# RWKV-5 and SwiGLU on one core: scores in four 64-column tiles, with half of the heads in swapped halves of time

## The chip, the cores and the metric

The kernel runs on one core of one Trainium2 chip. A core has five engines that run beside each other: TensorE (PE in the profile; PEld are its weight loads), VectorE (DVE), ScalarE (ACT), GpSimd (POOL) and SyncE (SP), whose queue issues most of the DMA transfers. They meet through semaphores. SBUF and PSUM have 128 partitions[...]. The metric is the time of one execution on the device, in microseconds, as the median of several runs. The time before is 603.12 us, the median of three (602.46 to 603.63).

## The reference

Two parts, one after the other, all in float32. Batch 4, 8 heads, 768 steps, 48 values a head:

```
for t in range(768):                       # attention, for each batch b and head h
    cur   = (u * k[t]) outer v[t]
    y[t]  = r[t] @ (state + cur)
    state = w * state + k[t] outer v[t]    # w: one decay for each head and key index
x = y as (4*768, 8*48)                     # 3072 tokens of 384
g = x @ w_gate;  val = x @ w_val           # 384 x 1536 each
out = (g * sigmoid(g) * val) @ w_out       # 1536 x 384
```

Within 128 steps the recurrence is a masked product. With k and r scaled by powers of w, `scores[key, query] = sum_d k[key, d] r[query, d]` for key before query, plus a diagonal from u; `y = scores^T v + r @ state`.

## The kernel before, in words

**Units.** The work of attention is cut into 24 units, unit `i` being 128 steps (`c = i // 4`) of one batch (`b = i % 4`). All 8 heads of a unit stand side by side, in four pairs `a`; head `2a + e` has the partitions `64e` to `64e + 47` once it is turned.

**A unit's way.** `load` and `load_v` fetch k, r and v with step on the partition, one transfer on SP for k, one for r, two for v. POOL scales k and r with two tables, `kscale` and `rscale`, that have step on the partition (`scale_k` L307, `scale_r` L310), and makes the unscaled product of r and k for the diagonal (`own_product` L234, L235; summed on VectorE by `own_sum` L240). From unit 12 on (`BLOCKS`) turning is not TensorE's: `move_blocks` (L364) issues 16 transfers on SP that move 32x32 blocks from SBUF to SBUF into one pair of buffers, and `turn_blocks` (L379) lets VectorE transpose 32x32 blocks twice, for k and for r. There is one such pair of buffers, so the moves of the next unit wait for the transposes of this one. `scores` (L393) then multiplies keys and queries of each head, 8 matmuls of 48 rows x 128 columns of weights and 128 moving columns, the even heads into one PSUM bank and the odd heads into another; `copy_predicated` (L398, VectorE) copies what lies above the diagonal under a mask into `At`, whose diagonal ScalarE has written (L328). `outputs` (L426) multiplies with v and with the state Z, in column tiles of 32: 28 matmuls; `update` (L441) makes the state's new part.

**Order.** The order of every engine is written out by hand (`manual_schedule`): a stage `s` scales unit `s + 1`, issues its loads and those of `s + 3`, turns unit `s`, makes the scores of `s - 1` and, from stage 12 on, right behind them the outputs and the update of `s - 2`. Between these stand pieces of the feed-forward block from a list `todo`, which `gaps` spreads over the stages. In odd stages the loads of `s + 3` stand on SP ahead of the moves, in even ones (`late`) behind them. The products of the feed-forward block are TensorE's main work: gate and value at first plainly (`gate_value`, L464), from the third group on in a scheme with fewer products, 15 rounds (`three_step`, L720) whose sums and differences VectorE, ScalarE (L744, L854) and POOL (L650, L623) make; the output projection (`project`, L539) in one of seven products. `three_beside` runs these rounds between the units in PSUM banks from the list `free`, `three_units` runs them after the last unit and takes banks of the pool `ps_a` too.

**PSUM.** Eight banks: four named ones for the feed-forward block, and a pool `ps_a` of four, from which scores, outputs, updates and transposes take theirs in rotation. `copy_predicated` is put off in a list, `lazy`.

Of the kernel before, what the change touches and what calls it, by code (L numbers as in the profile page):

```python
# [22 lines left out]
def fast(  # L23
# [39 lines left out]
    ps_a = ctx.enter_context(tc.tile_pool(name="ps_a", bufs=4, space=bass.MemoryType.PSUM))  # L63
# [8 lines left out]
    bad = cst.tile([P, HP], FP32, name="bad")  # L72
    held = cst.tile([P, HP], FP32, name="held")
    badc = cst.tile([P, 1], FP32, name="badc")
    ones = cst.tile([P, 1], FP32, name="ones")
    ident = cst.tile([P, P], FP32, name="ident")
    mask = cst.tile([P, P], FP32, name="mask")
# [12 lines left out]
    free = deque(banks[:2])  # L90

# [25 lines left out]

    def load(i):
        c, b = divmod(i, B)
        rows = slice(P * c, P * (c + 1))  # L120
        for src, dst in zip((k, r), raw(i)):
            sp.dma_start(out=dst, in_=src[b, :, rows, :].rearrange("h t d -> t h d"))

    def load_v(i):
        c, b = divmod(i, B)
        rows = slice(P * c, P * (c + 1))
        for e in range(2):
            sp.dma_start(
                out=v_ld[i % 4][:, :, 64 * e : 64 * e + D],
                in_=v[b, :, rows, :].rearrange("(a e) t d -> e t a d", e=2)[e],  # L130
            )
# [133 lines left out]
    def warm(n):  # L265

        ps = ps_a.tile([P, HP, P], FP32, name="warm", tag="a")
        for _ in range(n):
            pe.matmul(ps[:, 0, :], ident[:], ident[:], start=True, stop=True)
# [6 lines left out]
        base=0, pattern=[[1, P]], channel_multiplier=-1,  # L276
    )
    dve.tensor_scalar(held[:], wcol[:], W_LOW, W_HIGH, ALU.max, ALU.min)
# [33 lines left out]
    def natural_tables():  # L312
        for t, dst in ((pw[:, :, 1 : P + 1], kscale), (pv, rscale)):
            t_ps = ps_a.tile([P, HP, P], FP32, name="t_ps", tag="a")
            for a in range(HP):
                pe.transpose(t_ps[:, a, :], t[:, a, :], ident[:])
            act.copy(dst, t_ps[:].rearrange("p a (e x) -> p (a e) x", e=2)[:, :, 0:D])
# [25 lines left out]
    def turn(i):  # L343
        kr = khat[i % 4], rhat_of(i)
        tps = [ps_a.tile([P, HP, P], FP32, name="tp", tag="a") for _ in kr]
        turned[i] = three.tile([P, HP, P], FP32, name="rT", tag="rT")
        for tp, t, dst, table in zip(tps, kr, (kT[i % 2], turned[i]), (pw[:, :, 1 : P + 1], pv)):
            for a in range(HP):
                pe.transpose(tp[:, a, :], pair(t, a), ident[:])  # L349
            if i < 4:  # L350
                dve.tensor_mul(dst[:], tp[:], table)
            else:
                act.copy(dst[:], tp[:])
# [31 lines left out]
    def scores(i):  # L385

        while lazy:
            lazy.popleft()()
        ps = [ps_a.tile([P, HP, P], FP32, name="s_ps", tag="a") for _ in range(2)]
        for a in range(HP):  # L390
            for e in range(2):
                rows = slice(64 * e, 64 * e + D)
                pe.matmul(  # L393
                    ps[e][:, a, :], kT[i % 2][rows, at(i, a), :], turned[i][rows, at(i, a), :],
                    start=True, stop=True, skip_group_check=True,
                )
        for e in range(2):
            lazy.append(lambda e=e: dve.copy_predicated(  # L398
                At[i % 2][:].rearrange("p (a e) t -> p a e t", e=2)[:, :, e],
                mask[:].bitcast(INT32).unsqueeze(1).to_broadcast([P, HP, P]), ps[e][:],  # L400
            ))
        lazy.popleft()()
        if i < BLOCKS:
            lazy.popleft()()

    def outputs(i):

        c, b = divmod(i, B)  # L410
        A, vl, z = At[i % 2], v_ld[i % 4], Z[b]
        rT = turned.pop(i)
        ps = ps_a.tile([P, CC, P], FP32, name="y_ps", tag="a")
        cols = [[] for _ in range(4)]
        for m in range(4 * CC):
            (cc, q), (a, s) = divmod(m, 4), divmod(m, 3)
            each = [(z[0:R2, a, 32 * s : 32 * s + 32], rT[0:R2, at(i, a), :])] if c > 0 else []
            if s < 2:
                each.append((vl[:, a, 32 * s : 32 * s + 32], A[:, 2 * a, :]))
            if s > 0:  # L420
                each.append((vl[:, a, 32 * s + 16 : 32 * s + 48], A[:, 2 * a + 1, :]))
            cols[q] += [(cc, x, n == 0, n == len(each) - 1) for n, x in enumerate(each)]
        for n in range(len(cols[0])):
            for q in range(4):
                cc, x, start, stop = cols[q][n]
                pe.matmul(  # L426
                    ps[32 * q : 32 * q + 32, cc, :], *x,
                    start=start, stop=stop, skip_group_check=True,
                )
        act.copy(xT[:, i % NX, :, :], ps[:])  # L430

    def update(i):
# [4 lines left out]
        ps = ps_a.tile([P, HP, D], FP32, name="u_ps", tag="a")  # L437
# [398 lines left out]
    def three_units(g):  # L836
# [8 lines left out]
        def bank(chain):  # L845
            return wide[chain][:]

        def open_(chain):
            if chain in ("l4", "l2"):
                return take()  # L850
            return ps_a.tile([P, 4 * P], FP32, name=f"c_{chain}", tag="a")

        def later(at, do, out, *args):
            todo.append((at, lambda: do(out, *(bank(a) if isinstance(a, str) else a for a in args))))  # L854

# [9 lines left out]
        for t in range(4):  # L865
# [16 lines left out]
            later(z + 9.6, act.copy, y, "y")  # L882
            later(z + 10.4, dve.tensor_add, c[5], q10, "l5")
            later(z + (11.55 if t == 3 else 10.5), dve.tensor_add, c[2], y, "l1")
# [3 lines left out]
            later(z + r4, dve.tensor_sub, c[1], "l1", x)  # L888
            later(z + r4 + 0.1, dve.tensor_sub, c[1], c[1], "l8")
            later(z + r0, dve.tensor_sub, c[2], c[2], "l2")  # L890
            todo.append((z + r0 + 0.05, lambda: free.append(wide["l2"])))
            later(z + 11.6, dve.tensor_sub, c[0], r12, "n")
            silu(z + 10.8, 0, room["c"][:, 2], hTs[:, :, 3 * t + 2], pool, z + 10.9)
# [158 lines left out]
    for s in range(4, N + 2):  # L1052
        if 4 < s < N:
            own_sum(s)
        late = BLOCKS < s + 1 < N and s % 2 == 0
        if s + 1 < N:
            scale_k(s + 1)
            if not late:
                scale_r(s + 1)
            own_product(s + 1)  # L1060
            load_v(s + 1)
            if s + 3 < N and not late:
                load(s + 3)
# [30 lines left out]
        if s == 12:  # L1094

            dve.tensor_tensor(bad[:], held[:], wcol[:], ALU.not_equal)
            dve.tensor_reduce(badc[:], bad[:], axis=AX.X, op=ALU.add)
            dve.memset(ones[:], 1.0)
            n_ps = ps_a.tile([P, HP, P], FP32, name="n_ps", tag="a")
            pe.matmul(n_ps[0:1, 0, 0:1], badc[:], ones[:], start=True, stop=True)  # L1100
            act.copy(outside, n_ps[0:1, 0, 0:1])
# [426 lines left out]
```

## Time and profile before

| | |
|---|---|
| median of the runs | 603.12 us (602.46 to 603.63) |
| the profiled execution | 602.26 us, its span 600.4 us |
| granted TensorE clock | 0.999 |
| TensorE, its weight loads | 586.4 us (98%), 528.0 us (88%) |
| VectorE, ScalarE, POOL | 404.7 us (67%), 227.8 us (38%), 312.7 us (52%) |
| scores (L393), matmuls | 384 records, 28.2 us busy |
| outputs (L426), matmuls | 768 and 480 records, 34.9 and 29.8 us busy |
| update (L441), matmuls | 640 records, 10.1 us busy |
| block moves (L364) | 192 transfers of 32 KB, 2.0 us to landing |
| loads of k, of r (k_ld, r_ld), of v | 20, 20 and 48 transfers; 3.3, 3.7 and 3.5 us to landing |

The page says for each group of instructions its line, engine and operation, what it writes and reads, its shape and number, then its busy time, the mean length of one in ns, and the idle time of the engine before it with what ended it. For TensorE "48*128 48x128" is weights of 48 rows and 128 columns and a moving operand of 48 rows and 128 columns. Matmuls are pipelined, and a row's mean length is longer than the distance from one to the next; what a stretch costs is read from the chain, which follows the last instruction back through what released it. A float32 matmul leaves two records.

### The profile page before, as it was taken

The numbers are of one execution on the slowest core, as the hardware profiler recorded it, in microseconds if no ns is written. First come the engines' busy times: TensorE is split into PE (matmuls) and PEld (weight loads), VectorE is DVE, ScalarE is ACT, GpSimd is POOL, SyncE is SP. The second block draws the span as 40 slices with busy tenths as digits, with TensorE's granted clock in tenths as the row PEclk, the third lists the DMA queues.
The fourth block names the chain that finished last, engine by engine and source line by source line (L and its number), as shares of the span: only waits on it lengthen the run. The fifth ranks groups of instructions, "written<-read, shape, count | busy, mean of one in ns | idle before, by whom it ended". The sixth has DMA issues, their size and how long they took to land.

```text
span 600.4 us, 12410 instructions
## 1 busy us (share of the span) xinstructions
PE 586.4 (98%) x4920; PEld 528.0 (88%) x4920; DVE 404.7 (67%) x682; ACT 227.8 (38%) x524; POOL 312.7 (52%) x349
## 2 busy tenths in 40 slices
PE   8799999999999999999999999999999999999996
PEld 7578888899988889988899988889988899988896
DVE  5867886359477877477869477869347686277660
ACT  3358887321353422253441244432134421243310
POOL 4879888987999501977710988404445200011000
PEclk9999999999999999999999999999999999999999
DMA  7989883241530503133251253200100000000001
GB/s 174 236 210 246 228 289 84 44 73 40 115 47 8 97 3 75 37 66 53 34 93 24 68 88 49 36 2 1 41 14 0 2 1 26 27 1 1 2 0 58
DMA packets 138003, 40.43 MB, mean 67 GB/s; under 512 B 128592, under 2 KB 131792, under 8 KB 137936
## 3 DMA queue, kind: packets, MB, share of 16 engines
q1 hardware_dynamic: 134480, 34.82, 27.3%
q10 hardware_dynamic: 3456, 4.72, 2.2%
q8 instruction: 41, 0.67, 0.5%
q14 instruction: 26, 0.21, 0.1%
HBM read 28.51 MB, written 4.72 MB: 55 GB/s over the span
## 4 chain that ended last, share of the span: by engine, by line
PE 88%; POOL 2%; DVE 2%; issue 1%; DMA 1%; ACT 0%; SPq 0%; DVEq 0%; POOLq 0%
PE bank L720 31%; PE bank L539 26%; PE bank L464 7%; PE c_l L720 6%; PE y_ps L426 6%; PE c_n L720 3%; PE c_y L720 3%; PE s_ps L393 3%; POOL wgv L222 1%; PE u_ps L441 1%; PE tp L349 1%; DMA r_ld<-in_r_dram 1%; DVE hv L744 1%; DVE hs L513 0%; POOL hats L310 0%
## 5 line engine op out<-in xcount | busy, mean ns | idle before, releaser
L744 DVE TENSOR_TENSOR hv<-hv,bank 128x512 f32<-128x512 f32 x132 | 88.1, 683 | 29.6 <-PE bank L720 19.3
L464 PE MATMUL bank<-xT,wgv 128*128 128x256 f32 x288 | 66.8, 385 | 0.6 <-ACT xT L430 0.6
L328 ACT ACTIVATE At<-ident,du 128x128 f32<-128x128 f32 x176 | 60.3, 396 | 15.6 <-DVE hv L552 7.5
L720 PE MATMUL bank<-xf,wgv 128*128 128x256 f32 x256 | 66.0, 382 | 0.0
L860 POOL TENSOR_TENSOR hv<-At,hats 128x512 f32<-128x512 f32 x8 | 10.2, 1274 | 107.1 <-ACT At L859 107.1
L744 ACT COPY hv<-bank 128x512 f32<-128x512 f32 x72 | 40.2, 585 | 59.5 <-PE bank L720 50.5
L464 PEld LDWEIGHTS bank<-xT,wgv 128*128 128x128 f32 x288 | 53.2, 190 | 8.9 <-ACT xT L430 0.8
L650 POOL TENSOR_TENSOR s<-wgv 128x256 f32<-128x256 f32 x39 | 30.0, 793 | 53.4 <-PE bank L539 53.2
L720 PEld LDWEIGHTS bank<-xf,wgv 128*128 128x128 f32 x256 | 47.8, 190 | 7.0 <-DVE kT L854 0.6
L539 PE MATMUL bank<-wo,hv 128*128 128x192 f32 x288 | 49.6, 327 | 0.0
L398 DVE COPY_PREDICATED At<-mask,s_ps 128x512 f32<-128x512 int32 x48 | 34.3, 741 | 20.6 <-ACT At L328 13.8
L539 PEld LDWEIGHTS bank<-wo,hv 128*128 128x128 f32 x288 | 47.2, 190 | 0.6
L539 PE MATMUL bank<-wt,hs 128*128 128x192 f32 x240 | 42.1, 327 | 1.2 <-DVE hs L513 1.2
L545 ACT COPY hv<-bank 128x192 f32<-128x192 f32 x36 | 11.3, 316 | 83.9 <-PE bank L539 83.9
L539 PE MATMUL bank<-wo,hs 128*128 128x192 f32 x240 | 42.5, 327 | 0.0
L539 PEld LDWEIGHTS bank<-wt,hs 128*128 128x128 f32 x240 | 39.3, 190 | 2.1 <-issue 1.1
L539 PEld LDWEIGHTS bank<-wo,hs 128*128 128x128 f32 x240 | 39.5, 190 | 0.5 <-DVE hv L547 0.3
L751 ACT ACTIVATE hv<-hv 128x512 f32<-128x512 f32 (+1 forms) x33 | 21.1, 668 | 48.6 <-DVE hv L744 48.6
L426 PE MATMUL y_ps<-At,v_ld 128*32 128x128 f32 x768 | 34.9, 273 | 1.4 <-DVE At L398 1.4
L720 PE MATMUL bank<-xT,wgv 128*128 128x256 f32 x144 | 35.6, 380 | 0.0
L720 PE MATMUL bank<-xT,s 128*128 128x256 f32 x152 | 35.2, 380 | 0.0
L454 POOL TENSOR_TENSOR Z<-Z,w 48x192 f32<-48x192 f32 x32 | 17.3, 540 | 33.3 <-DVE Z L453 32.1
(203 smaller groups left out, 1299.8 us busy)
## 6 DMA issues: line engine op xcount, KB each, us to landing
hats<-hats SPq DMA_DIRECT2D x192, 32.0 KB, 2.0
w_bits<-in_moe_w_gate_dram SPq DMA_DIRECT2D x6, 768.0 KB, 6.6
v_ld<-in_v_dram SPq DMA_DIRECT2D x48, 96.0 KB, 3.5
w_bits<-in_moe_w_val_dram SPq DMA_DIRECT2D x6, 768.0 KB, 6.0
w_bits<-in_moe_w_out_dram SPq DMA_DIRECT2D x6, 768.0 KB, 6.1
out_dram<-hv ACTq DMA_DIRECT2D x24, 192.0 KB, 1.9
k_ld<-in_k_dram SPq DMA_DIRECT2D x20, 192.0 KB, 3.3
r_ld<-in_r_dram SPq DMA_DIRECT2D x20, 192.0 KB, 3.7
```

Of the source, the lines that this page charges most:

```text
L328: lambda h=h: act.activation(At[i % 2][:, h, :], ident[:], AF.Identity, scale=du[:, h : h + 1])
L393: pe.matmul(ps[e][:, a, :], kT[i % 2][rows, at(i, a), :], turned[i][rows, at(i, a), :], start=True, stop=True, skip_group_check=True,)
L398: lazy.append(lambda e=e: dve.copy_predicated(At[i % 2][:].rearrange("p (a e) t -> p a e t", e=2)[:, :, e], mask[:].bitcast(INT32).unsquee ...
L426: pe.matmul(ps[32 * q : 32 * q + 32, cc, :], *x, start=start, stop=stop, skip_group_check=True,)
L454: pool.tensor_mul(ze, ze, w)
L464: pe.matmul(gv[:, o, :].rearrange("p (i t) -> p i t", i=2), wt[:, c, P * f : P * (f + 1)], xT[:, 2 * g % NX : 2 * g % NX + 2, c, :], start ...
L539: pe.matmul(ps, lhs[:, f, :], rhs[:, f, :], start=(f == 0 and n in (0, 1, 4)), stop=(f == FH - 1), skip_group_check=True,)
L545: act.copy({0: o1[:, 0:NH], 2: o1[:, NH:DM], 3: o2[:, NH:DM]}[n], ps)
L650: op(made[o], made[a], made[b])
L720: pe.matmul(ps[:, o], u[:, o], v, start=first and o == 0, stop=True, skip_group_check=True,)
L744: do(out, *(pair_of(wide[a][:]) if isinstance(a, str) else a for a in args))
L751: todo.append((at, lambda: act.activation(gate, gate, AF.Silu)))
```

## The change

From unit 12 on (`SWAPPED`):

- The scores of a pair of heads are computed in four tiles of the array, 64 rows x 64 columns each. For pairs 0 and 1, keys 0 to 63 go with all 128 queries, and keys 64 to 127 only with queries 64 to 127: the quarter in which every key comes after every query is left out. 16 matmuls in place of 8, of 128 and of 64 moving columns.
- Pairs 2 and 3, four heads of the eight, stand in swapped halves of time: steps 64 to 127 on partitions 0 to 63, and the other way round. There it is the right column half that has 128 queries and the left that has 64. `load` and `load_v` fetch each of their transfers in three pieces to bring this about; the two tables are swapped once for these heads, by two transfers on SP in stage 10 and a copy on POOL in stage 11; the mask gets a second plane for them; and `outputs` reads the moving columns of these heads as two runs of 64, the second run first.
- The pool `ps_a` of four rotating tiles becomes four named tiles in a ring that the kernel turns itself (`next_psum`). In `three_units` a chain takes the first of the ring, and gives it back (`back`) once it is read.

The core of the diff:

```diff
+    ring_a = deque(ps_a.tile([P, 4 * P], FP32, name=f"ring{n}") for n in range(4))
+
+    def next_psum(m, n):
+        t = ring_a[0]
+        ring_a.rotate(-1)
+        return t[:, 0 : m * n].rearrange("p (a x) -> p a x", a=m)
...
+    SWAPPED = 12
+
+    def places(i, n):
+
+        if i < SWAPPED:
+            return [(slice(0, P), slice(0, n), 0)]
+        return [
+            (slice(0, P), slice(0, n // 2), 0),
+            (slice(0, 64), slice(n // 2, n), 64),
+            (slice(64, P), slice(n // 2, n), -64),
+        ]
+
     def load(i):
         c, b = divmod(i, B)
-        rows = slice(P * c, P * (c + 1))
         for src, dst in zip((k, r), raw(i)):
-            sp.dma_start(out=dst, in_=src[b, :, rows, :].rearrange("h t d -> t h d"))
+            for p, h, o in places(i, H):
+                rows = slice(P * c + p.start + o, P * c + p.stop + o)
+                sp.dma_start(out=dst[p, h], in_=src[b, h, rows, :].rearrange("h t d -> t h d"))
...
+    pool.memset(mask[0:64, 1, 64:P], 0.0)
+    pool.memset(mask[64:P, 1, 0:64], 1.0)
...
-        ps = [ps_a.tile([P, HP, P], FP32, name="s_ps", tag="a") for _ in range(2)]
-        for a in range(HP):
+        ps = [next_psum(HP, P) for _ in range(2)]
+        whole, left, right = slice(0, P), slice(0, 64), slice(64, P)
+        if i < SWAPPED:
+            parts = [(a, whole, whole) for a in range(HP)]
+        else:
+            parts = []
+            for a in range(HP // 2):
+                parts += [(a, left, whole), (a, right, right)]
+                parts += [(a + HP // 2, right, whole), (a + HP // 2, left, left)]
+        for a, keys, cols in parts:
             for e in range(2):
                 rows = slice(64 * e, 64 * e + D)
                 pe.matmul(
-                    ps[e][:, a, :], kT[i % 2][rows, at(i, a), :], turned[i][rows, at(i, a), :],
+                    ps[e][keys, a, cols],
+                    kT[i % 2][rows, at(i, a), keys], turned[i][rows, at(i, a), cols],
                     start=True, stop=True, skip_group_check=True,
                 )
...
+            dst = At[i % 2][:].rearrange("p (o a e) t -> p o a e t", o=2, e=2)[:, :, :, e]
+            m = mask[:].bitcast(INT32).unsqueeze(2).to_broadcast([P, 2, HP // 2, P])
+            dve.copy_predicated(dst, m, ps[e][:].rearrange("p (o a) t -> p o a t", o=2))
...
+        def in_order(x, a):
+            if i < SWAPPED or a < HP // 2:
+                return x
+            return bass.AP(
+                tensor=x.tensor, offset=x.offset + 64,
+                ap=[list(x.ap[0]), [-64, 2], [1, 64]],
+            )
...
-            return ps_a.tile([P, 4 * P], FP32, name=f"c_{chain}", tag="a")
+            return ring_a.popleft()
...
+        if s + 2 == SWAPPED:
+            halves_of = two.tile([P, H, D], FP32, name="swapped", tag="rk")[:].rearrange(
+                "p (n h) d -> p n h d", n=2
+            )
+            for p, o in ((slice(0, 64), 64), (slice(64, P), -64)):
+                sp.dma_start(
+                    out=halves_of[p], in_=scales[p.start + o : p.stop + o, 1:3, H // 2 : H]
+                )
+        if s + 1 == SWAPPED:
+            pool.tensor_copy(scales[:, 1:3, H // 2 : H], halves_of)
```

`load_v` is cut in the same way as `load`, and `outputs` passes its moving operands of k and of the state through `in_order`.

## The prediction

> **What bounds the kernel now.** I read the page's busy shares first, then its slices, then the chain that ended last, then that chain in order of time around one unit, then the groups of TensorE and of its weight loads by shape, and last the timelines of SP, POOL and VectorE where the change adds to them.
>
> The page's head, its busy shares, and the slices of TensorE:
>
> ```profile
> span 600.4 us, 12410 instructions
> ...
> PE 586.4 (98%) x4920; PEld 528.0 (88%) x4920; DVE 404.7 (67%) x682; ACT 227.8 (38%) x524; POOL 312.7 (52%) x349
> ...
> PE   8799999999999999999999999999999999999996
> ...
> PEclk9999999999999999999999999999999999999999
> ...
> PE 88%; POOL 2%; DVE 2%; issue 1%; DMA 1%; ACT 0%; SPq 0%; DVEq 0%; POOLq 0%
> ```
>
> TensorE is busy in nine tenths or more of every slice after the first 30 us, at full clock, and the chain is TensorE's for 88% of the span; what isn't lies before 58.6 us, but for two short stands (about 219 to 224 and 405 to 410 us). A busy TensorE is not one at its peak, so the question is what a unit's scores cost in the chain. One unit of the chain in order of time (start, length, what):
>
> ```profile
> 209.94 2.37 PE bank L720 x11
> 212.31 1.09 PE s_ps L393 x16
> 213.40 1.68 PE y_ps L426 x56
> 215.08 0.34 PE u_ps L441 x32
> 215.42 2.15 PE bank L539 x12
> ```
>
> Scores take 1.09 us, back to back with their neighbours; all twelve units from 12 on show the same 1.09. x16 are 8 matmuls, two records each: a float32 matmul runs in two passes. Time taken out of this row is taken out of the chain.
>
> **The scores' own time.** Two tiles of the array (the rows of the even and of the odd head) each stream 4 matmuls x 2 passes = 8 streams of 128 columns. How long a stream is, and whether column tiles run beside each other, the outputs' rows show, which have four column tiles of 32:
>
> ```profile
> 213.81 0.37 PE L426 MATMUL y_ps<-rT,Z 112*32 112x128 f32 x3
> ...
> 213.92 0.28 PE L426 MATMUL y_ps<-rT,Z 112*32 112x128 f32 x2
> ...
> 214.03 0.37 PE L426 MATMUL y_ps<-At,v_ld 128*32 128x128 f32 x3
> ```
>
> A round of four concurrent streams comes every 0.11 us (213.81, 213.92, 214.03), and 56 records / 4 = 14 rounds x 0.11 = 1.54 of the 1.68 us. So column tiles do run side by side, and a stream of 128 columns is 0.11 us. The scores are then 8 x 0.11 = 0.88 us and a head of 0.21 us (array standing between two shapes of tile, and the first weights, which nothing hides); the outputs' head is 0.14.
>
> ```profile
> L393 PEld LDWEIGHTS s_ps<-rT,kT 48*128 48x128 f32 x384 | 23.6, 187 | 6.0 <-issue 4.9 <-DVE At L398 0.6 <-ACT sgs L470 0.5
> ...
> L426 PEld LDWEIGHTS y_ps<-At,v_ld 128*32 128x32 f32 x768 | 30.3, 110 | 2.4 <-issue 1.4 <-DVE At L398 0.8
> ...
> L441 PE MATMUL u_ps<-v_ld,hats 128*32 128x48 f32 x640 | 10.1, 206 | 0.0
> ```
>
> The heads' difference of 0.07 is the weights': a load of 128 columns shows 187 ns, one of 32 columns 110.
>
> **The change, part by part.**
>
> *Scores in four tiles* (units 12 to 23). 16 matmuls instead of 8, weights of 64 columns. Each of the four tiles gets, over two pairs of heads, 2 x 2 streams of 128 columns and 2 x 2 of 64; the right half gets its short stream first, the left its long one, so both are free again together. A stream of 64 columns has no row. From below, the update's 48 columns: 32 records in 0.34 us are 8 rounds of 0.042. From above, 128 columns: 0.11. It is much nearer to 48; between them in proportion, 0.042 + 16/80 x 0.068 = 0.056. Tile: 4 x 0.11 + 4 x 0.056 = 0.66. Head: 64 columns of weights instead of 128, 64/96 x 77 ns less, 0.21 - 0.05 = 0.16. A unit: 0.82 instead of 1.09, gain 0.27; twelve units **-3.2 us**. Ends: 0.042 for a stream and 0.16 for the head give -3.9; streams held in strict order across tiles (each pair of heads then waits for its longest path, some 0.05 more a unit) give -2.6.
>
> Here a rule speaks against the change. The Trainium skill, "TensorE: Matmul & The Clock Gate", section "Wait — 56ns, not 53.3ns?", says that starts of matmuls are never closer than about 25 ns, however small they are. There are now 32 streams a unit, 0.80 us by that rule, so 0.96 with the head, and only 0.13 x 12 = 1.6 us gained. The update's row stands against it: 640 records in 10.1 busy us are 16 ns each, and in the chain 0.34 us / 32 = 11 ns. So tiles beside each other start closer than the rule has it in this very kernel; I take the row, and keep 601.5 as a rival. A second one, "TensorEngine Tiling (Array Packing)", section "Instruction Overhead", gives each matmul some 60 cycles and advises against cutting a short dimension; with 48 columns at 0.042 us a round that overhead isn't seen here between streams.
>
> *Outputs read half of their moving columns in swapped order* (14 of 28 matmuls, two runs of 64, the second first). No row has a negative step; the nearest is L720 on xT, whose moving operand is two separate runs of 128 columns: 0.86 us for 4 records in the chain, 0.84 ns a column, no more than the outputs' single runs (0.11 / 128). I take 0; 5 ns on each of some 7 rounds a unit would be 0.4 us in all.
>
> *copy_predicated with a mask of two planes*: still 128x512 from PSUM, and the row's mean is 741 ns; TensorE doesn't read that At before the next unit. 0; VectorE at 67% would bear 0.1 us more each.
>
> *Loads of k, r (2 to 6 transfers) and v (2 to 6) on SP.* Same bytes and packets. What it costs is SP's time, since the 16 block moves (L364) of the next unit stand in the same queue, and the two transposes (L379) on VectorE wait for them. The tightest place, SP then VectorE:
>
> ```profile
> 355.06 0.60 SPq L122 DMA_DIRECT2D k_ld<-in_k_dram  x1
> 355.70 0.59 SPq L122 DMA_DIRECT2D r_ld<-in_r_dram  x1
> 356.39 1.36 SPq L128 DMA_DIRECT2D v_ld<-in_v_dram  x2
> 361.33 10.76 SPq L364 DMA_DIRECT2D hats<-hats  x16
> ```
>
> ```profile
> 376.24 0.69 DVE L379 STREAM_TRANSPOSE kT<-hats 128x512 f32<-128x512 f32 x1
> ```
>
> About 0.6 us a transfer, whatever its size (16 moves of 32 KB in 10.76, one k of 192 KB in 0.60). 12 transfers instead of 4 are 7.2 us: 362.3 instead of 357.75, so the moves begin 1 us late. They end at 373.0, land 2.0 later (page, DMA issues), at 375.0; the transpose starts at 376.24 before, and about 2.8 earlier in the new kernel, when the loads too stand some 2.5 earlier. VectorE waits 0 to 1.5 us there; its next instructions empty TensorE's banks, of which four stand between, at 0.86 us a round: hidden. In the stages where both loads stand between two sets of moves 18 transfers (10.8 us) replace 6: 155.5 to 166.3, where SP waited until 166.80; 262.1 to 272.9 plus its wait, against 276.72; 307.2 to 318.0, against 321.67 (2 us earlier in the new one). All fit, barely. k, r and v themselves are used a stage or more later. Cost 0, upper end 1.5 us.
>
> *Scales of four heads swapped once*: two transfers on SP at unit 10, a copy on POOL at 11 of 128x384, ahead of scale_k (115.70). It isn't in the trace; between a memset of that size (four in 1.48 at the start, 0.37) and L307 (1.00), I take 1.00. POOL is full until about 199 us, so all behind it is 1 us later: the moves of unit 12 start at 119.70 + 1.0 + 2.4 (four more transfers) = 123.1, end 11.7 later at 134.8 and land at 136.8; their transpose ran at 138.44. POOL's forms (L650) for TensorE are written 8 us and more before their use (the last of one group at 166.23, read from about 177). Hidden: 0.
>
> *The mask's second plane, three more small steps on POOL at the start*: under 1 us, inside the 3.97 us in which POOL waits for r. 0.
>
> *PSUM ring by hand instead of the pool*: the same rotation of four in the units; in the tail a bank goes back when read, so l8 may take y's bank instead of n's. TensorE runs there without stands in the chain. 0.
>
> Sum: -3.2 us on the profiled execution's 602.26 (its span 600.4 and 1.9 around it), 599.1 for it. The median shown is 603.12, 0.9 above: **599.9 us**. The two stands at 219 and 405 keep it: their chain starts from TensorE (L744 waits for its bank), so they move along.
>
> **Rivals.**
>
> *The starts are the limit*, by the rule above: 603.1 - 1.6 = 601.5.
>
> *SP's queue takes it back* (slower). Place: stages 13, 19 and 21. If small loads take 1.2 us each, as one r did (1.16 at 159.01), 18 take 21.6 and 12 take 14.4: in stage 13 the moves are 10.6 us late against 7.6 of room, VectorE stands 3.0; in 19 and 21 about 6.5 each. That is 16, less some 3 of cover each (the banks' 4 x 0.86), 7 on TensorE: 603.1 - 3.2 + 7 = 607. It decides from about 0.95 us a transfer. For it: 207 us of other waits fill SP's list, but L364 waits for L379 85.8 us in 9 places, which is room; against: the usual 0.6.
>
> *The halves take turns*: if left and right of a row group didn't overlap, 2 x 0.66 + 0.16 = 1.48 a unit, +0.39 x 12: 607.8. The outputs' and the update's rounds speak against it.
>
> *Nothing comes of it*: TensorE reaches waits for VectorE and ScalarE sooner, and stands: 603.1. For it, VectorE and ScalarE follow closely in places (L744 waits for TensorE only 20.7 us in 65 places); against, both have a third of their time free.
>
> **How the numbers follow.** Forecast 0.60, starts as the limit 0.12, nothing 0.11, SP 0.13, halves in turn 0.04. A measurement of this kernel tells about 0.2%, 1.2 us. Faster: 0.60 + 0.12 = 0.72; same 0.11; slower 0.17. The likeliest alone: 599.0 to 600.9. The range runs from 598.8 (-3.9 and a little) over the starts and the unchanged case to 603.6, and leaves SP's and the halves' cases out.
>
> **What would show it.** The chain's scores at about 0.82 us with 32 records from unit 12 on, the outputs at 1.68, transposes starting without a wait for DMA, two loads of a stage in 3.6 us on SP. Wrong if scores stay above 0.95, if L379 waits for DMA and TensorE's bank rows show stands behind it, or if the outputs' row grows.

## The result and the profile after

The changed kernel takes 599.29 us, the median of seven runs (599.13 to 601.73), against 602.46 us for the kernel before beside it: ratio 0.9950, 95% interval 0.9936 to 0.9964, 3.0 us faster. The prediction was 3.2 us faster, from a median of 603.12. A second measurement on another chip gave 599.02 against 601.80 us, ratio 0.9954 (0.9941 to 0.9967). The profiled execution took 599.74 us, its span 598.0 us, 2.4 us less than the span before.

The sum came out, but not by its own terms: the scores gained what was forecast, a stand (TensorE idle, waiting) took more than half of that back in the profiled execution, and a part that the prediction had at nothing, where tiles lie in SBUF, brought about as much as the stand took. That the two cancel is luck.

The page of the changed kernel, its head, the slices of TensorE and the shares of the chain:

```profile
span 598.0 us, 12924 instructions
...
PE 582.6 (97%) x5112; PEld 524.4 (88%) x5112; DVE 405.0 (68%) x682; ACT 228.0 (38%) x524; POOL 313.6 (52%) x352
...
PE   8799999999999999999999999899999999999996
...
PE 83%; POOL 4%; DVE 3%; SPq 2%; issue 1%; DMA 1%; ACT 1%; POOLq 0%; DVEq 0%
```

TensorE's share of the chain fell from 88% to 83%, POOL's rose from 2% to 4%, and SP's queue, 0% before, has 2%. One slice of TensorE, the 26th (374 to 389 us), went from 9 to 8. Both say that something stands that did not stand before.

The same unit in the chain as shown of before (start, length, what), and the scores' groups by shape:

```profile
210.34 0.81 PE ring L423 x24
211.15 1.69 PE ring L476 x56
212.84 0.34 PE ring L491 x32
```

```profile
L423 PE MATMUL ring<-rT,kT 48*64 48x128 f32 x192 | 10.8, 277 | 0.0
L423 PE MATMUL ring<-rT,kT 48*64 48x64 f32 x192 | 10.5, 223 | 0.0
...
L423 PEld LDWEIGHTS ring<-rT,kT 48*64 48x64 f32 x384 | 9.0, 133 | 3.7 <-issue 3.7
```

Scores are 0.81 instead of 1.09 us (the chain follows 24 of the 32 records), outputs 1.69 instead of 1.68, the update is unchanged. The weights of 64 columns show 133 ns, between the 110 of 32 columns and the 187 of 128.

**Where the time went.** I follow the start of the outputs (the rows of 56 records) along the chain, after minus before. At the first it is 57.15 - 58.60 = -1.45, before any of the changed units. From 132 us on it falls by about 0.27 with each unit, to -1.45 at 131.65, -2.25 at 211.15, -3.04 at 283.37, -3.31 at 330.82 and -3.57 at 350.94. Two units later it is -2.21, and at the last outputs, 432.07 against 434.53, -2.46. So: start -1.45; twelve scores -3.3; outputs +0.1; one stand between 351 and 393 us +1.9; a small one between 306 and 314 us +0.3.

The size of the large stand: from 350.94 to 393.33 are 42.39 us. Before, the same way was 354.51 to 395.54 = 41.03, with two scores of 1.09; with two of 0.81 it would be 40.47. So 1.92 us are lost there. It is in these lines of SP's timeline of the changed kernel (start, length, what, number):

```profile
352.21 1.96 SPq L141 DMA_DIRECT2D k_ld<-in_k_dram  x3
354.21 1.90 SPq L141 DMA_DIRECT2D r_ld<-in_r_dram  x3
356.22 3.88 SPq L148 DMA_DIRECT2D v_ld<-in_v_dram  x6
360.20 12.50 SPq L386 DMA_DIRECT2D hats<-hats  x16
```

and in POOL's:

```profile
370.14 0.73 POOL L700 TENSOR_TENSOR s<-s 128x256 f32<-128x256 f32 x1
374.48 1.00 POOL L332 TENSOR_TENSOR hats<-r_ld,scales 128x384 f32<-128x384 f32 x1 [3.62 <-DMA hats<-hats]
375.44 1.17 POOL L700 TENSOR_TENSOR s<-s,wgv 128x256 f32<-128x256 f32 x1
```

SP issues k, r and v until 360.10, so the 16 moves of unit 22 cannot start at 357.71, when VectorE has transposed unit 21. They last 12.50 us, and the last, issued at 372.09, lands 2.00 later. POOL's scale of r for unit 23 (L332) writes the buffer that these moves read; it waits 3.62 us for their landing, and the sums and differences (L700, the forms) that TensorE's next products need are behind it in POOL's order. The chain of the changed kernel goes that way, and TensorE's own row names what it waited for (1.64 of the 1.92 us show there as idle time):

```profile
372.09 2.00 DMA hats<-hats
...
374.48 1.00 POOL hats L332
375.49 1.83 POOL s L700 x2
...
377.38 15.13 PE bank L770 x68
392.51 0.81 PE ring L423 x24
```

```profile
377.38 1.97 PE L770 MATMUL bank<-xT,s 128*128 128x256 f32 x8 [1.64 <-POOL s L700]
```

Before, the same scale (L310 there) ran at practically the same moment, without a wait, and TensorE did not stand: it came later.

```profile
374.38 1.00 POOL L310 TENSOR_TENSOR hats<-r_ld,scales 128x384 f32<-128x384 f32 x1
```

VectorE's transpose waited too (1.95 us, at 374.48), but TensorE did not stand for that.

### The profile page after: what moved, and what is told of

The parts are those of the page before. It is cut to its first block, busy times and chain, and to the rows that moved or that the text cites. A ratio compares the mean times of both kernels' runs of the same rounds, so it can differ in the third digit from the quotient of the medians.

```text
span 598.0 us, 12924 instructions
## 1 busy us (share of the span) xinstructions
PE 582.6 (97%) x5112; PEld 524.4 (88%) x5112; DVE 405.0 (68%) x682; ACT 228.0 (38%) x524; POOL 313.6 (52%) x352
## 4 chain that ended last, share of the span: by engine, by line
PE 83%; POOL 4%; DVE 3%; SPq 2%; issue 1%; DMA 1%; ACT 1%; POOLq 0%; DVEq 0%
PE bank L770 28%; PE bank L589 26%; PE ring L770 13%; PE bank L514 7%; PE ring L476 5%; PE ring L423 2%; SPq L386 2%; POOL wgv L242 1%; POOL s L700 1%; DVE hv L794 1%; PE ring L491 1%; PE ring L371 1%; DMA r_ld<-in_r_dram 1%; DVE hs L563 1%; POOL hats L332 0%
## 5 line engine op out<-in xcount | busy, mean ns | idle before, releaser
L794 DVE TENSOR_TENSOR hv<-hv,bank 128x512 f32<-128x512 f32 x132 | 88.0, 683 | 29.1 <-PE bank L770 18.7
L794 ACT COPY hv<-bank 128x512 f32<-128x512 f32 x72 | 40.2, 586 | 61.3 <-PE bank L770 55.0
L700 POOL TENSOR_TENSOR s<-wgv 128x256 f32<-128x256 f32 x39 | 30.0, 793 | 53.1 <-PE bank L589 53.0
L476 PE MATMUL ring<-At,v_ld 128*32 128x128 f32 x768 | 34.9, 273 | 1.5 <-DMA v_ld<-in_v_dram 1.5
L770 PEld LDWEIGHTS bank<-xT,s 128*128 128x128 f32 x152 | 28.6, 190 | 6.4 <-POOL s L700 2.0
```

What stands on the lines that cost most here:

```text
L476: pe.matmul(ps[32 * q : 32 * q + 32, cc, :], *x, start=start, stop=stop, skip_group_check=True,)
L700: op(made[o], made[a], made[b])
L770: pe.matmul(ps[:, o], u[:, o], v, start=first and o == 0, stop=True, skip_group_check=True,)
L794: do(out, *(pair_of(wide[a][:]) if isinstance(a, str) else a for a in args))
```

## The experiments

Every row names the median, that of the kernel before beside it, the ratio with its 95% interval, and from the profile the start of the first outputs, the way from there to the last outputs ("stretch"), and the scores' row. All times in us.

| kernel | median | before | ratio | first outputs | stretch | scores |
|---|---|---|---|---|---|---|
| before | | | | 58.60 | 375.93 | 1.09 |
| changed | 599.29 | 602.46 | 0.9950 (0.9936-0.9964) | 57.15 | 374.92 | 0.81 |
| changed, second measurement | 599.02 | 601.80 | 0.9954 (0.9941-0.9967) | 57.01 | 374.27 | 0.81 |
| changed, whole scores | 600.46 | 601.79 | 0.9980 (0.9971-0.9989) | 56.49 | 375.95 | 1.09 |
| before, loads cut | 601.70 | 601.79 | 0.9999 (0.9990-1.0008) | 59.36 | 376.21 | 1.09 |
| changed, v behind the moves | 598.84 | 601.79 | 0.9943 (0.9930-0.9957) | 56.83 | 374.76 | 0.81 |
| before, ring by hand | 601.73 | 601.79 | 0.9996 (0.9987-1.0005) | 58.07 | 375.94 | 1.09 |
| before, places in SBUF | 601.41 | 602.56 | 0.9977 (0.9964-0.9991) | 57.28 | 375.92 | 1.09 |
| before, 64 bytes further | 601.92 | 601.80 | 1.0005 (0.9996-1.0013) | 58.43 | 375.96 | 1.09 |
| before, 128 bytes further | 602.05 | 601.80 | 1.0001 (0.9992-1.0009) | 58.39 | 375.93 | 1.09 |
| changed, quarter computed | 601.40 | 602.56 | 0.9974 (0.9961-0.9988) | 56.82 | 375.85 | 1.03 |
| changed, halves in turn | 602.73 | 602.56 | 1.0000 (0.9987-1.0013) | 57.15 | 377.27 | 1.21 |
| changed, v behind in every second stage | 598.48 | 602.56 | 0.9921 (0.9900-0.9942) | 58.07 | 373.05 | 0.81 |
| the same, 32 bytes further | 597.80 | 601.80 | 0.9928 (0.9915-0.9941) | 57.87 | 373.06 | 0.81 |

The first outputs differ by up to 1.6 us between profiles of kernels with the same places in SBUF (56.49 to 58.07), for a reason that wasn't found; the stretch doesn't, and the medians average over it.

**Whole scores.** The changed kernel with the old 8 matmuls, everything else kept.

```diff
-        if i < SWAPPED:
+        if True:
             parts = [(a, whole, whole) for a in range(HP)]
```

> The changed kernel with the scores of units 12 to 23 whole again: 8 matmuls of 128 keys by 128 queries a unit, the quarter above the diagonal computed too; the halves in swapped order, both masks, the split loads and the ring stay as in the changed kernel. My theory (the gain is the shorter scores): the scores' row goes back from 0.81 to 1.09 us in the chain, TensorE comes some 3.3 us later to the last units, of which the stand of some 1.6 us at the forms of unit 23 hides a part: 600.7 to 602.6 us, 1.4 to 3.3 over the changed kernel. Rival (the gain comes from elsewhere, the start or the ring): within 0.5 us of the changed kernel.

Measured 0.9980, by the ratios 1.6 to 1.8 us over the changed kernel: inside the difference that I expected. The scores' row is 1.09 again:

```profile
351.33 1.09 PE ring L423 x16
352.42 1.68 PE ring L476 x56
```

Its stretch, 375.95, is that of the kernel before, 375.93, to 0.02: swapped outputs, masks, loads and ring cost nothing in it, and the stand is gone although SP has all its loads, because TensorE isn't early: POOL's scale runs 21.73 us behind the outputs' row at 352.42, against 23.54 behind the one at 350.94 in the changed kernel. But the kernel is 1.2 us faster than the kernel before (interval 0.7 to 1.7), all of it ahead of the first outputs. I had no reason for that.

**The loads alone.** The kernel before with k, r and v cut in three pieces from unit 12 on, heads not swapped.

```diff
...
-            sp.dma_start(out=dst, in_=src[b, :, rows, :].rearrange("h t d -> t h d"))
+            for p, h in places(i, H):
+                rows = slice(P * c + p.start, P * c + p.stop)
+                sp.dma_start(out=dst[p, h], in_=src[b, h, rows, :].rearrange("h t d -> t h d"))
```

> The kernel before with the loads of k, r and v of units 12 on cut in three pieces each (6 transfers become, with v, 12 more a unit pair of stages), heads not swapped, nothing else changed: SP's longer queue alone. My theory: without the 3.3 us by which the shorter scores bring TensorE ahead, SP's lateness stays hidden, or nearly: 0 to +0.5 us over the kernel before, the moves of unit 22 begin near 361 us, and POOL's scale of r of unit 23 waits for them, but TensorE does not stand for it more than 0.5 us. Rival (SP's queue costs a fixed 1.6 us or more, wherever TensorE is): +1.5 to +2.5 us.

As my theory had it: no difference in the medians, 0.28 us in the stretch. POOL does wait for the moves there,

```profile
377.46 1.00 POOL L322 TENSOR_TENSOR hats<-r_ld,scales 128x384 f32<-128x384 f32 x1 [2.27 <-DMA hats<-hats]
```

and TensorE stands 0.26 us for it (355.29 to 396.58 are 41.29, before 41.03). SP's longer queue alone is hidden; it costs when TensorE comes early. The kernel with the quarter computed is between: its scores bring TensorE ahead by only 0.06 a unit, and it loses 0.5 at the same place.

**v behind the moves.** In stage 12 and on, the six transfers of v for unit `s + 1` come behind the moves of that unit.

```diff
-            load_v(s + 1)
+            if s < SWAPPED:
+                load_v(s + 1)
...
             move_blocks(s + 1)
+            if s >= SWAPPED:
+                load_v(s + 1)
```

> The changed kernel with the six transfers of v of the next unit issued behind the 16 block moves of that unit instead of ahead of them, from stage 12 on. My theory (the moves of unit 22 are late because SP is still issuing v): the moves start some 3.9 us earlier, POOL's scale of r of unit 23 waits 3.6 us less, TensorE's stand of 1.6 us before the last units is gone: 597.5 to 598.2 us, 1.1 to 1.8 under the changed kernel. Rival (what holds POOL there is not SP but the moves' own time on the queue or the POOL's forms): no change within 0.5 us; or v lands too late for the outputs and it gets slower.

Missed: 0.9943 isn't told apart from the changed kernel's 0.9950 and 0.9954, and the stand is still 1.72 us. The edit doesn't do what I wrote. With v shifted in every stage, the v of unit 21 comes behind the moves of unit 21, and that is ahead of the moves of unit 22: six transfers left the place and six others came in. SP's timeline has them ahead of k and r, and the moves begin at 359.33, only 0.87 us earlier.

**v behind the moves in every second stage.** The edit that takes six transfers out of that place, and brings the places with 18 transfers down to 12.

```diff
-            load_v(s + 1)
+            if s < SWAPPED or s % 2 == 0:
+                load_v(s + 1)
...
             move_blocks(s + 1)
+        if SWAPPED <= s < N - 1 and s % 2:
+            load_v(s + 1)
```

> The changed kernel with the six transfers of v of the next unit issued behind the 16 block moves of that unit in every second stage only (13, 15, ... 21); in the stages between they stay ahead of the moves. Shifting them in every stage left as many transfers between two sets of moves as there were: 12 between those of units 21 and 22. This one leaves 6 there, and 12 instead of 18 in the stages that had 18. My theory (the moves of unit 22 stand behind SP's loads): they start at about 357.5 instead of 360.2 us, POOL's scale of r of unit 23 runs some 2.5 us earlier, TensorE's stand of 1.9 us before unit 22's scores is gone: 1.5 to 2.2 us under the changed kernel, 4.5 to 5.2 under the kernel before. Rival (POOL's own list, or the moves' length, sets that stand): within 0.5 us of the changed kernel.

SP, POOL and the chain of this kernel:

```profile
352.46 1.96 SPq L141 DMA_DIRECT2D k_ld<-in_k_dram  x3
354.46 1.90 SPq L141 DMA_DIRECT2D r_ld<-in_r_dram  x3
358.73 11.77 SPq L386 DMA_DIRECT2D hats<-hats  x16
370.61 8.44 SPq L148 DMA_DIRECT2D v_ld<-in_v_dram  x12
```

```profile
372.76 1.01 POOL L332 TENSOR_TENSOR hats<-r_ld,scales 128x384 f32<-128x384 f32 x1 [0.94 <-DMA hats<-hats]
```

```profile
367.06 0.81 PE ring L423 x24
367.88 1.69 PE ring L476 x56
369.57 22.00 PE bank L770 x100
391.57 0.81 PE ring L423 x24
```

SP now has a gap ahead of the moves: they wait for the transposes of unit 21, not for SP. POOL waits 0.94 instead of 3.62 us, and TensorE runs 22.00 us without a stand, as the kernel before does. From 351.88 to 392.38 are 40.50 us, against the 40.47 without loss. The stretch is 1.9 us shorter than in the first profile of the changed kernel and 1.2 shorter than in the second (where the stand was 41.73 - 40.47 = 1.26). By the ratios it is 1.7 to 2.0 us under the changed kernel; with the 32 bytes of a later experiment, on one chip with it, 597.80 against 599.02. So what took the gain back was SP's list ahead of the moves of unit 22. This version is the fastest of all, 4.3 to 4.8 us under the kernel before.

TensorE is 0.94 us later in this profile than in the first of the changed kernel (351.88 against 350.94), which might have hidden part of the stand. It is not what did it. Take in each kernel the time from that outputs' row to POOL's scale of r for unit 23, and the loss in the way to the outputs two units on:

| kernel | outputs to POOL's scale | loss | difference |
|---|---|---|---|
| changed | 23.54 | 1.92 | 21.62 |
| v behind the moves | 23.36 | 1.72 | 21.64 |
| changed, second measurement | 22.88 | 1.26 | 21.62 |
| changed, quarter computed (scores 0.22 longer) | 22.39 | 0.54 | 21.85 |
| before, loads cut (scores 0.28 longer) | 22.17 | 0.26 | 21.91 |
| changed, halves in turn (scores 0.40 longer) | 22.00 | 0 | |
| changed, whole scores (scores 0.28 longer) | 21.73 | 0 | |
| v behind in every second stage | 20.88 | 0.03 | |
| before | 19.87 | 0 | |

Up to 21.62 us, plus what the scores in between are longer, next to nothing is lost, and beyond it all is, to 0.03 us. The lateness of POOL's scale, counted from TensorE's own row, is the whole of the stand.

**The ring by hand.** The kernel before with `next_psum`, `ring_a` and `back` alone.

> The kernel before with the PSUM ring turned by hand alone: the same four banks in the same order but for the tail. My theory: no difference, within 0.3 us of the kernel before. Rival (the 1.45 us by which the changed kernel is ahead at its first outputs come from the ring): about 1.4 us faster, with its first outputs at 57.2 instead of 58.6 us.

No difference, as expected; its stretch is 375.94. The start isn't the ring's.

**The places in SBUF.** What is left of the change ahead of the first outputs is the mask's second plane, and the diff makes room for it: `bad`, `badc` and `ones` become one tile. By the addresses in the built programs every tile behind the mask lies 448 bytes further in the changed kernel. So: the kernel before with that alone, and no instruction added.

```diff
-    bad = cst.tile([P, HP], FP32, name="bad")
...
-    badc = cst.tile([P, 1], FP32, name="badc")
-    ones = cst.tile([P, 1], FP32, name="ones")
+    counts = cst.tile([P, HP + 2], FP32, name="counts")
+    bad, badc, ones = counts[:, 0:HP], counts[:, HP : HP + 1], counts[:, HP + 1 : HP + 2]
...
-    mask = cst.tile([P, P], FP32, name="mask")
+    mask_tile = cst.tile([P, 2, P], FP32, name="mask")
+    mask = mask_tile[:, 0]
```

> The kernel before with the tiles placed in SBUF as the changed kernel has them: a mask of two planes of which the second is never written or read, and the three small tiles of the counts in one; not one instruction added. It is for the 1.3 us by which the changed kernel with whole scores is faster than the kernel before, all of it before the first outputs. Theory A (where the tiles lie changes how fast the first transfers land): 1.0 to 1.6 us under the kernel before. Theory B (POOL's longer mask steps or the order of instructions bring the start forward): no difference, within 0.4 us.

Theory A: 0.9977, 1.4 us under the kernel before (0.5 to 2.2), with the stretch unchanged at 375.92. The DMA view of the first transfers, from 2 to 34 us, says where. For the kernel before, then for this one (packets, MB, the time that the packets took as a share of 16 engines):

```profile
q1 hardware_dynamic: 17184, 6.88, 94.0%
```

```profile
q1 hardware_dynamic: 17184, 6.88, 88.1%
```

The same packets, the same bytes, and 6% of 32 us, 1.9 us, less time on each engine. The traces' packets say which: the 14336 of 192 bytes take 18.4 ns each on the mean before and 16.3 here, 1.8 us on each of 16 engines; those of 2048 bytes take 102 and 103 ns. All profiles fall into these two kinds: the kernel before, its ring and its cut loads have 94.0 to 95.9%, and every kernel that has the changed kernel's places has 87.8 to 90.7%.

**64 and 128 bytes further.** To find what in the shift it is, the kernel before with an unused tile ahead of the identity (32 columns instead of 16 for 128 bytes).

```diff
+    cst.tile([P, 16], FP32, name="gap")
     ident = cst.tile([P, P], FP32, name="ident")
```

> The kernel before with 64 unused bytes a partition ahead of the identity, so that every tile from there on lies 64 bytes further; nothing else. In the kernel before, the buffer that the first four units' k and r land in (runs of 192 bytes, 256 apart) starts 96 bytes past a multiple of 128; in the changed kernel and with its layout alone it starts 32 past one; all of them 32 past a multiple of 64. Theory A (it is where the runs fall within 128 bytes that matters: from 96 a run of 192 touches three such lines, from 32 only two): as the layout alone, 1.0 to 1.6 us under the kernel before. Theory B (the whole shift of 448 bytes matters, or other neighbours): within 0.4 us of the kernel before.

> The same with 128 unused bytes: the buffer starts 96 past a multiple of 128 again. Theory A (place within 128 bytes): no difference from the kernel before, within 0.4 us. Theory B (any shift does it): 1.0 to 1.6 us under it.

Theory A as I wrote it fell: 64 bytes bring nothing, though the runs then lie within 128 bytes as in the changed kernel. 128 bytes bring nothing either. The DMA view of the kernel with 64 bytes agrees with its time:

```profile
q1 hardware_dynamic: 17184, 6.88, 93.6%
```

So it isn't lines of 128 bytes. The buffer in which the first four units' k and r land holds runs of 192 bytes, 256 apart. Past a multiple of 256 it starts at 96 in the kernel before, 160 and 224 in these two, 32 in the changed kernel: from the first three every run crosses a multiple of 256, from 32 none does. The Trainium skill, "DMA: Bandwidth & Descriptors", section "How a descriptor splits into AXI transactions", has that boundary for what is read: a transaction starts at a multiple of 256 bytes, and a run that doesn't start on one costs the bytes from the boundary below as well. What moved here is the place written to, which that section leaves open. The number of transactions, two or one, fits all placements. The bytes from below don't show: they would give 9, 11 and 13 beats of 32 bytes for the runs from 96, 160 and 224, and those have 94.0, 93.6 and 94.0%, and 18.4, 18.2 and 18.1 ns a packet. The boundary would explain also why only the start gains: the later k, r and v land with runs 192 or 448 bytes apart, of which three in four cross a boundary before and after the change. That the boundary of 256 is the cause was read from these placements and is not shown: a shift of 192 bytes alone should bring the gain and wasn't made.

**32 bytes more.** The best version with the counts' tile 32 bytes longer.

> The changed kernel with v behind the moves in every second stage (as above) and the counts' tile 32 bytes longer, so that k, r and v land at 64 past a multiple of 128, a multiple of 64: a run of 192 bytes touches two lines of 128 and three of 64, not four. If lines of 128 alone count: no difference from the same without the 32 bytes, 4.5 to 5 us under the kernel before. If lines of 64 count too: another 0.3 to 1 us at the start.

0.9928 against 0.9921 without it: no difference that shows. The DMA view has 85.4%, the lowest of all,

```profile
q1 hardware_dynamic: 17184, 6.88, 85.4%
```

and its packets of 192 bytes take 15.4 ns, against 16.1 without the 32 bytes. That would fit again: from 64 past a multiple of 256 the first buffer's runs don't cross, and of the later ones two in four instead of three. In the time it isn't seen.

**The changed kernel beside it.**

> The changed kernel itself beside them on this chip, to set the parts against each other: by the sum of the parts (start -1.3 by the layout, scores -3.3, stands +2.2) it is 2.4 us under the kernel before; by its first measurement 3.0 (2.2 to 3.9).

2.8 us under the kernel before (2.0 to 3.6), between the two sums; its stand was 1.26 and not 1.92 us, which makes the sum of the parts 3.0.

**The quarter computed.** Four tiles of 64 columns as in the changed kernel, but 128 queries for both halves of keys.

```diff
-                parts += [(a, left, whole), (a, right, right)]
-                parts += [(a + HP // 2, right, whole), (a + HP // 2, left, left)]
+                parts += [(a, left, whole), (a, right, whole)]
+                parts += [(a + HP // 2, right, whole), (a + HP // 2, left, whole)]
```

> The changed kernel with all 128 queries for both halves of keys, so that the quarter above the diagonal is computed too (and masked off as before): four tiles of 64 columns stay, only the shorter streams are gone. My theory: 8 streams of 0.11 us a tile and the head of 0.16: 1.04 us a unit instead of 0.81, so the tiles alone bring 0.05 of the 0.28 us and the quarter left out brings the rest; TensorE 2.8 us later at the end of the units, of which the stand before unit 22 gives 1.6 to 1.9 back: 0.9 to 1.2 us over the changed kernel. Rival (64-column tiles themselves are what is faster): 0.9 us a unit or less and within 0.5 us of the changed kernel.

```profile
351.25 1.03 PE ring L423 x32
```

1.03 against 1.04 expected. Of the 0.28 us a unit, 0.06 come with the narrower tiles (by the forecast's working, from their shorter weights) and 0.22 with the shorter streams; by the ratios it is 1.2 to 1.5 us over the changed kernel, for 0.9 to 1.2 expected. Tiles of half the columns bring next to nothing for themselves; they are what makes it possible to leave out a quarter.

**Halves in turn.** The changed kernel's matmuls, in each unit all of the left half of keys first.

```diff
+        if i >= SWAPPED:
+            parts.sort(key=lambda p: p[1].start)
```

> The changed kernel with each unit's matmuls in another order: all 16 that write the left half of the keys (both row groups), then all 16 of the right half. Same matmuls, same tiles. My theory (a tile's matmul waits for its own tile, and those behind it in TensorE's queue wait with it): the halves no longer overlap but at the seam, 0.16 + 2 x 0.66 less one stream, 1.35 to 1.48 us a unit, 6 to 8 us over the changed kernel less the stand of 1.9: 4.5 to 6.5. Rival (each tile takes its own from the queue): 0.81 us a unit and no difference.

```profile
394.09 1.21 PE ring L425 x27
```

Neither: 1.21 us, not 1.35 to 1.48 and not 0.81; 2.8 to 3.0 us over the changed kernel, for 4.5 to 6.5 expected. The records of one unit, told apart by the lengths of their streams, have the right half's first stream at 268.190, when the left half has begun the fifth of its eight streams in each row group (268.178). So, if the lengths tell the halves apart rightly, the right half neither waits for the left's last matmul nor starts with its first: here TensorE took a matmul for a free tile from some way down its list, and not from any distance. Alternating the halves is worth 0.40 us a unit.

## Why the prediction came out

**The scores**: right, by its terms. Forecast 0.82, measured 0.81 (12 x 0.28 = 3.3 for 3.2). Its streams for a tile, four long and four short, are those of four pairs of heads, not of two as it says. The records have a stream of 64 columns every 0.055 us (forecast 0.056), one of 128 every 0.11. The head of 0.16 holds too: with all queries 8 x 0.11 + 0.16 = 1.04 for a measured 1.03.

**Starts as the limit** (601.5): wrong. 32 starts lie within 0.67 us, 21 ns each on the mean, and the tiles of one round start 6.5 ns apart. The rule of the Trainium skill, "TensorE: Matmul & The Clock Gate", section "Wait — 56ns, not 53.3ns?", about 25 ns from start to start, does not hold for tiles side by side, and was rightly put behind the update's row.

**Loads on SP at 0, upper end 1.5**: this step failed. The place was the one named, the moves of unit 22, and the transfers took 0.65 us each instead of 0.60, so that the moves began at 360.20. But I asked who waits for the moves on VectorE only. The moves read a buffer too, and POOL's scale of r for unit 23 writes it: POOL stood 3.62 us, the forms behind it were late, TensorE stood 1.3 to 1.9. The rival "SP's queue takes it back" had the right queue and the wrong follower; its price, 7 us, was that of transfers of 1.2 us. And the cover was TensorE's own lateness: before, POOL was ready at the same moment and nobody waited. The gain itself used up the cover. One of the signs of being wrong came half true: the transpose did wait for DMA, 1.95 us, and a stand of TensorE came with it, but by POOL. "Same bytes and packets" was off by 1536 packets (134480 before, 136016 with the loads cut), which cost nothing in that kernel's median.

**The mask at start, 0**: wrong, and in a direction in which I didn't look. Its three steps on POOL are hidden (POOL still waits 3.04 us for r). The price of the second plane is paid in addresses, and was a gain of about 1.4 us (0.5 to 2.2, by the places alone): a term that stood nowhere in the sum, and that made up for the stand.

**The other steps.** Outputs: 0.01 us a unit longer, 0.1 in all, for 0; with whole scores, in the same swapped order, they take the old 1.68, so the order isn't what costs it. The mask of two planes in `copy_predicated`: nothing (stretch of the kernel with whole scores). POOL's copy of the scales: 0.51 us instead of the 1.00 that I took. The ring: 0. "Nothing comes of it", by TensorE reaching waits sooner: true for 0.3 us, between 306 and 314 us, where the chain goes over VectorE (L794, L563). The reading of the chain left out its end: from 595.07 us on it wasn't TensorE's before either. "The halves take turns": no, but in the other order they partly do.

So the time, 599.29 for 599.9, is right by 3.3 - 1.9 - 0.3 - 0.1 + 1.4 = 2.4 us in the profiled execution, where the sum had 3.2 and nothing else.

## What to carry to other kernels

When a change makes the bounding engine faster, recompute every wait at the times of the new kernel: cover that consists of that engine's own lateness goes away with the gain, and a queue that is only longer (0.0 us alone) costs 1.3 to 1.9 us together with it. For a step that is late, follow both those who read its result and those who are to overwrite what it reads. And compare where tiles lie before and after: an added tile can move the landing places of transfers that the change never touches, so measure the layout alone before a gain is put down to the work.

## What was not expected of the hardware

**Where short runs land.** The 17184 packets of the start take 93.6 to 95.9% of the engines' time where the first buffer's 192-byte runs cross a multiple of 256 bytes, and 85.4 to 90.7% where they don't; some 1.4 us of this kernel. A packet of 192 bytes takes 18.1 to 18.8 ns in the first and 15.4 to 16.3 in the others.

**Order among tiles side by side.** With the halves in turn, a matmul for a free column tile started ahead of another that stands before it in the list: 268.190 for the right half's first, 268.399 and 268.454 for the left half's last in the same rows. The streams' lengths alone tell the halves apart.

**TensorE's slow start.** The same 36 first records, ahead of any data, take different times, in the profiles of before and after:

```profile
2.84 7.02 PE L269 MATMUL warm<-ident 128*128 128x128 f32 x36 [2.84 <-POOL ident masks.py:199]
```

```profile
2.85 6.08 PE L289 MATMUL ring<-ident 128*128 128x128 f32 x36 [2.85 <-POOL ident masks.py:199]
```

Their records come every 213 ns at first and every 112 ns later; the step is at 8.55 us in the one and 6.64 in the other. The view prints a granted clock of 1.00 there, but the traces hold no clock record ahead of the step: the first begins, at full clock, at 8.60 and 6.64 us, and within 0.07 us of the step in all fourteen profiles. The stretches at full clock last 587.09, 590.51 or 593.92 us, 3.41 apart. The Trainium skill, "TensorE: Matmul & The Clock Gate", section "What's actually happening", has a gate that opens after activity in a free-running window of about 3.4 us; that fits both, and a step whose moment changes from one execution to the next.

Over all profiles the row is 5.96 to 7.07 us, in kernels of both kinds, but it does not set the first outputs: in the second profile of the changed kernel it is 6.96, 0.88 longer than in the first, and the first outputs are 0.14 earlier (57.01); the shortest row, 5.96, goes with 58.43. What moves the first outputs beyond the places in SBUF stays open, a reason to read a start from several profiles and the medians, not from one.
